# Layer B's sliding attention moved from VectorE products to tiled matmuls over runs of 32 keys

## The chip, the cores and the metric

The kernel runs on one core of one Trainium2 chip. The metric is device time of one execution in microseconds. A core has engines that work side by side and wait for each other by semaphores: TensorE (PE) for matmuls, with weight loads shown apart as PEld; VectorE (DVE) for elementwise work; ScalarE (ACT) for activations and copies; GpSimd (POOL); and SyncE (SP), whose queue issues the DMAs. TensorE writes to PSUM, eight banks of 512 float32 columns on 128 partitions, and DVE or ACT carry results from there to SBUF. On this core each engine runs its own instructions in the order in which they were written.

## The reference

Four residual layers A, B, A, B on one sequence of 2048 positions, 512 channels, 32 heads of 16. Layer A is linear attention with a learned feature map; the change touches layer B, in which each position attends to eight positions: itself and those 2, 4, ... 14 before it.

```python
x = x + _A_ref(_layernorm(x, axis=-1), A_wqkv, A_w_phi, A_wo)
x = x + _B_ref(_layernorm(x, axis=-1), B_wqkv, B_wo)
x = x + _A_ref(_layernorm(x, axis=-1), A_wqkv, A_w_phi, A_wo)
x = x + _B_ref(_layernorm(x, axis=-1), B_wqkv, B_wo)

def _B_ref(x, wqkv, wo):                       # S = 2048, H = 32, Dh = 16
    W, dil = 8, 2
    q, k, v = ...                              # x @ wqkv, by head
    idx = pos[:, None] - (jnp.arange(W) * dil)[None, :]
    mask = idx >= 0
    kg, vg = ...                               # k and v at idx: (B, H, S, W, Dh)
    logits = jnp.einsum("bhsd,bhswd->bhsw", q, kg) * Dh ** -0.5
    logits = jnp.where(mask[None, None, :, :], logits, -1e9)
    attn = _softmax(logits, axis=-1)
    o = jnp.einsum("bhsw,bhswd->bhsd", attn, vg)
    return o.transpose(0, 2, 1, 3).reshape(B, S, D) @ wo
```

## The kernel before

The sequence is cut into four blocks `b` of 512 positions, each of four tiles `t` of 128. Both rounds `L` of the layers use the same weights, held in SBUF. The stages of one round are: `s_a1` (keys and values of layer A, their features, and the running sum `kv` over all four blocks), `s_a2` (query features), `s_akv` (the finished sum turned into weights, once a round), and then for each block `s_a3` (normalisers), `s_a4` (layer A's output), `s_b1`, `s_b2`, `s_b3` (layer B). `s_out` ends both layers: four matmuls of 512 columns per tile against the output weights (L520), and the residual. The residual is added in one of two ways: by a fifth matmul with the identity and an eviction on ACT (L523, L530), or by DVE (L533). Then come sums of squares and the normalisation for the next layer.

Every step goes through `step` (a named thread of one engine) or `flex` (a copy that may run on DVE or ACT). `_ORDER`, a list of thread names written out by hand or by a search, says in which order the steps are emitted, and so the order on each engine; `_CHOICE` has one digit for each flexible step (DVE or ACT; for the residuals, identity matmul or DVE); `_SLOTS` names the buffer that each tile takes. There is no scheduler at run time.

Layer B, per block:

- `s_b1`: 48 matmuls of 512 columns at L927 give Q, K and V with channels on partitions, each a weight block of every fourth column of `WB` (so that one partition holds one head's channel). ACT or DVE evict each 128x512 result (L190, L192). POOL adds a halo of 16 positions from the block before (L953, L965, L969). Then `vrep` makes 16 DMAs (L988) that copy V, shifted, into `Vg`.
- `s_b2`: `prod` (L1019), four DVE products of 128x4096 of Q with eight shifted views of K; `lgt` (L1026), 32 matmuls with the 0/1 weights `indQK` on four column tiles of 32, which sum the channels; `ex` (L1033), two exponentials; `den` (L1042), two matmuls that sum the eight exponentials; `rd` (L1047, L1049), logarithm and exponential for the reciprocal; `pt` (L1054), the normalised weights.
- `s_b3`: `pav` (L1081), four DVE products of 128x4096 of these weights with views of `Vg`; `mo` (L1090), 32 matmuls with `indAV` that sum over the window; four evictions; `s_out`.

A matmul can use a part of the 128x128 array, given by `tile_position`: a shape such as 128x32 (rows x columns) leaves four tiles that are used in turn. L668 (`kv`) uses two tiles of 128x64, L714 (`ms`) and L782 (`md`) four of 128x32, L900 sixteen of 32x32, L808 four of 32x128.

At the start `warm` puts 14 matmuls on a zeroed tile `kvT` (L242, L287). In layer A four more blocks write and read DRAM for `rho` (L824, L831), the only round trips through DRAM of this kernel.

Of the kernel before, what the change touches and what calls it, by code (L numbers as in the profile page):

```python
# [8 lines left out]
BF16 = mybir.dt.bfloat16  # L9
# [20 lines left out]
KVW = 16 + TB  # L30
VGW = 3 * KVW + TB + 8
# [5 lines left out]
_BUFS = {"big": 8, "med": 16, "t2": 6, "ps": 8}  # L37
# [3 lines left out]
    "fold_dma": (),  # L41
    "half_k": ((0, 3), (1, 3)),
    "half_ln": (),
    "split": ((1, 2), (1, 3)),
    "v_dram": (),
    "half_mo": (),
    "rho_pad": 0,
# [10 lines left out]
av 8 i i i i i i i i i i i i 0 f 0 g e 2t 0 bs 9 h a d c 0 j k t i i j l 27 o p 3 3 d6 b 1x 1x t 1y o m 2 2 1q  # L58
1z 1x 1x q u t r 1q v x w n s 1r w 1s 4 20 y 21 1x 22 1x 23 1q 1q 1q 1q 1v 1w z 3d 3d 3d 1u 1t 25 3e 3e 3e z 5
3e 3e z z 26 10 18 18 d5 1 z 16 11 4i 15 6 1h 13 3d 3e 3e 25 25 26 18 25 18 12 26 26 28 26 26 26 26 19 12 28  # L60
2a 28 1h 18 14 12 12 1a 28 1c 3e 2g 2g 1f 2h 2h 1h 1h 1b 1i 2b 1b 1e 1d 29 2j 2k 1h 1j 1n 2r 1b 1l 2s 1b 2c 2r
1k 2s 17 2g 2g 2h 2h 1k 1k 2h 2h 2h 2h 2d 1g 2d 2d 2d 2e 2j 1m 35 36 32 2o 2o 33 2s 33 32 33 33 2r 2s 2s 1o 2o
2o 2d 2r 3a 1k 3a 1p 2p 2o 24 24 2s 24 2u 2v 35 37 2u 2u 2u 2s 2i 2w 2j 3a 2s 3a 2l 2z 2j 24 32 32 34 2m 3b 33
3d 3f 3f 2z 2z 2z 33 2f 33 33 2f 2f 2f 3a 3a 2q 2q 2q 30 3a 2n 3a 3a 2z 3e 2q 2x 35 35 b6 3b 3a 2y 31 31 31 31
3c 3c 38 3c 39 3c 3m 3f 3n 3o 3o 3o 24 24 3g 3g 3g 3f 3p 3q 3g 3g 3g 3g 3g 3r 3q 3f 3g 24 3h 3i 3i 5l 5m 5n 3p
3s 3q 3j 3k 3k 3t 3q 3p 3x 5m 3w 3u 3h 3i 3i 3q 3v 3q 3q 3y 3h 3i 3q 3i 3h 3i 3q 5l 5o 5p 5r 5m 5q 7 7 3z 3q
3i 3j 3k 5m 5l 5s 3k 7 7 5m 5m 5m 3h 3i 7g 40 5u 44 41 42 5t 5m 5m 3j 3j 7h 7i 3k 5v 5m 5w 43 7h 45 7j 45 60
3k 3k 3k 46 45 45 5y 5x 5z 61 61 48 47 47 61 49 47 4a 47 4b 62 47 4b 63 3j 4g 94 4c 45 4d 45 4e 4f 3k 45 45 61
64 63 4h 4p 65 95 7j 7j 66 4q 63 96 95 97 97 63 67 7h 63 67 69 7h 6b 4k 4k 4k 4l 4p 4r 4k 4m 4p 4p 4s 4t 7k 7n
6a 68 6c 4o 7m 50 50 4u 4u 4u 4n 4u 7l 4w 97 7o 7p 7p 7q 7s 3l 4x 7r 7r 7p 7t 7p 6o 7u 50 7r 7r 7v 6o 6j 4v 4y  # L70
4j 6o 6q 6o 4j 4z 6k 6p 6r 6j 7r 6e 6l 95 6d 95 7v 6t 6s 6f 6d 7w 6e 7z 7x 98 9b 9a 99 6g 7y 9c 6e 6j 6j 9d 9d
6u 9d 6e 6n 80 6m 9d 6h 6v 6v 9e 9h 9f 6i 9g 9f 6w 6v 6v 6w 6w 9f 9i 9f 87 88 8h 9j 9f 50 82 9j 9l 6w 6x 6x 87
87 6w 81 83 9n 6x 9k 87 8b 89 51 51 51 51 52 52 8c 8c 8e 6u 6u 6u 9m 8j 8a 8d 8c 6v 6y 3l 8f 82 9o 82 85 82 50
51 52 4z 4z 4z 9q 9q 9s 8c 6z 8g 6y 6z 9r 71 70 6y 6y 6z 6z 72 86 a0 a0 a1 73 84 8i 74 75 74 74 50 74 8i 76 8i
77 a2 76 79 53 53 54 55 54 a5 56 53 54 9v 78 76 9q 9q 76 a0 81 53 9v 9w 9p 7a 57 9v 9u a7 76 7a 9t 8j 7c 9y 54
58 59 59 59 9v 59 9x 7d 7e 5a 8j 8j 7b 7f 5c 5b 5d 5b 5b a0 8k 5e 5b 5f 8k 9z a7 5b 5f 5j 8k 8k 8l a3 5i b4 a4
b7 5h b4 b4 b4 8l 5g b5 b5 a7 b5 b5 a7 8k 8l 8j c3 8i c3 b8 c4 c4 c4 c4 a8 8m a8 a8 a8 c3 a9 a9 5k at c1 b5 a6
8m au au c1 c2 b5 c2 aw c2 c2 a8 a9 b5 b5 8n 8o 8n 8p 8m at au at at 8n 8q 8m a7 aa 8n aw 8r 8s au au au 8s 8s
8t au au 8s 8v a6 a6 8u aa 8w aa 8x 8u 8u 8u 8y ab ac ab ad a6 aa b7 8u b9 b7 c3 8y 90 92 c1 91 c1 c2 8z c2 c2
aw ay ab c2 ba ae ab af aw b0 c4 c4 b1 bc ag ag ag ag ah bc aj ak bc c1 c4 c4 bc al ax c3 ai ai ai bd b1 ai am  # L80
93 bf bi bg az bf ai am ar bf bf bg bg aq b7 bg bg bg bg bg bb an ao ag ag ap bi ag ag b1 b1 bc b2 c2 bi bn bi
bl bk as bq br br bq br br bq bq b1 br by by by by bt b3 b3 b3 b3 br be be be br br bz c5 c5 bh bj bn bn bn c5
bu c4 by by by by c6 bo by c6 c6 c5 bt bt bt bn bv c6 c6 c6 bz be bp bp bw bm bp bp c0 c0 by c6 c6 bx c0 c0 c9
c5 ca c6 cb cb cc cb cd ce cd fr fs c7 c8 c7 c8 c8 ft cc ci cf cd cg cd c7 c8 c8 fs fu c8 e2 fu ch cd e3 cd cc
cj ck e4 cd c7 c8 c8 c7 e3 e2 cm cd c8 e6 e7 fu cl cd cd cn cp co e5 e3 hb e3 cr e2 ea e9 cq hc cs e3 cs e8 e3
e3 hd eb ec e3 e3 e3 ed ct cv hc eh cs he ee cs ef cw eg ei cx ei ei cu ei cu cu cu fs cy fs fv ej cu cy d0 cz
ek d2 fw fx fz d3 cs cs fy cs cs g0 g0 g0 el ek em ek en ek d4 d1 dc g1 eo ek g2 g3 g2 dc de eo es g0 g4 dd dh
g2 g5 g2 he hc eq g6 d7 d8 d7 d7 d7 he di dc g2 dc d9 ep er hc et dn hf da db df dh dh dh hi hh hj hg hk hk hk
dj dk dl dm dm g6 g7 g9 dn dn dg ga f0 f0 hl hm hn hm ho hm ev ew f1 hk dn g8 do do hp f2 fa fc hm hq do do dp
ev ex fc gb ev f0 dp ey dn f3 f0 hm fc f4 hq ev ez fc do dp dn dq dq d6 f5 f6 dm dm eu hs gi gj gi fd gs hr fd  # L90
ht fd hu hv fd dq fe fe f5 f5 f8 f5 f9 f7 fb gk fd fe fc gn gn gp gi gi gl gm gd gd gd ge ic gf i7 i7 i9 gg i8
dr dr dt ds dr du hx hy gd dq gu dr dv gn gq gh i7 ff ia gu fb go ff fg fh fb fb eu gv gc gn i2 gr i3 hx hz hx
i7 i2 ib gv i4 hx i1 gc hw i2 i2 i5 gu i0 gu gv gv gw gt ie fg fi if i6 ie id gw if dw dx id gv gw id id ie ie
if if ig dw ff ig if ig fg fj dw e0 dw ff fg fk ie fl fm fl fn gu fl fl fp ih ih ih ih e1 ii ii ii ik ij fq dy
gt gt gt fo fo il io io io io ii im ip iq ip is ir ir ih ii in ip ip iu it ir gx ir gy gx gx gx gz gy h0 dz dz
iv gy h1 h4 gx gy h2 h4 iw iv h5 h5 h6 h7 gy h4 h3 h5 h8 h9 h7 h7 h4 h5 ha h7
# [4 lines left out]
    "0011111111111001110111111010000010010000000000000001011111101100100000110101000110000010000001110111"  # L101
    "1101011110010000110101000000000000001101011000000000100100000000000000000101111100000011011000000000"
    "0000000000001101111010000000100101011111010000011001110111000000000000000111111011101110010100101000"
    "00000000000001111001000000000000000000000000000000000000000000000000000000000001111"
)


_SLOTS = {
    "big": (
        "0123456701231231456204632073205712053720457604356704213560421356720415763215063506432506"  # L110
    ),
    "med": (
        "0123456789abcdef5837ae98eeaeae471853bc9e43cbe47199ce3185413cebf94c8f74e3581bc71931bc7f370bf9ac21584e"
        "af9c37214a0b589dec37"
    ),
    "t2": (
        "0123450123450342150132451032451032451032451302153421530421503452014520345123045130425123504321504321"
        "5043215043210451023134"
    ),
    "ps": (  # L120
# [9 lines left out]
class _Fast:  # L130

    def __init__(self, ctx, tc, A_x, A_wqkv, A_w_phi, A_wo, B_wqkv, B_wo, out):
# [16 lines left out]
        for n in ("xn", "xnT", "oT", "Eq", "rS", "kvp", "K", "QT", "Vg", "PT", "vh"):  # L149
            setattr(self, n, {})  # L150
# [1667 lines left out]
```

## Time and profile before

| what | value |
|---|---|
| median of 3 runs | 329.74 us (329.51 to 329.87) |
| profiled execution, first to last instruction (its span) | 327.5 us |
| TensorE clock granted over the span | 0.998 |
| PE / DVE / ACT busy | 310.3 / 302.2 / 279.3 us |
| layer B projections, L927, 384 matmuls | 87.6 us of PE |
| `lgt` L1026 and `mo` L1090, 528 matmuls | 34.1 us of PE |
| `prod` L1019 and `pav` L1081, 66 products | 145 us of DVE |

The span is what the profiled execution's page counts; the runs' times hold some 2 us more than it. Busy time is what an engine spent in instructions; the groups by line give it for each line and shape, with the number of instructions and the mean duration of one. Matmuls are pipelined, so the duration of one (380 ns for 512 columns) is longer than the distance to the next; the distance is read from start times or from a run of many in the chain of waits.

### The profile page before, as it was taken

How to read it: one execution, taken by the hardware profiler on the slowest of the kernel's cores; microseconds unless marked ns; L12 is line 12 of the kernel's file. 1: busy time of each engine (PE TensorE's matmuls, PEld its weight loads, DVE VectorE, ACT ScalarE, POOL GpSimd, SP SyncE). 2: the span in 40 equal slices, each digit the busy share in tenths (PEclk: the TensorE clock that was granted, in tenths of full speed). 3: DMA queues.
4: the chain of work that ended last, by engine and by line, in shares of the span. 5: the costliest groups of instructions: out<-in, count | busy, mean ns of one | idle time of the engine just before them, and what ended most of it. 6: DMA issues, size and time to landing. Idle time of an engine off the chain costs nothing. (4 is left out here: it accounts for less than half of the span.)

```text
span 327.5 us, 8033 instructions
## 1 busy us (share of the span) xinstructions
PE 310.3 (95%) x3176; PEld 149.5 (46%) x3203; DVE 302.2 (92%) x439; ACT 279.3 (85%) x634; POOL 25.3 (8%) x50
## 2 busy tenths in 40 slices
PE   7999999999999999999999999979999999999873
PEld 3655456445444444443444455644544454433221
DVE  7998995998998999899999999699999999999993
ACT  5999988998888999989999999798999996676550
POOL 4000000000021003000000000000000208400000
PEclk9999999999999999999999999999999999999999
DMA  7980000004556899998750300023436977679952
GB/s 197 380 197 3 0 2 4 2 20 120 105 148 135 152 164 133 139 121 154 137 135 1 67 3 2 4 59 90 128 58 125 179 146 134 150 139 158 166 176 92
DMA packets 37388, 35.41 MB, mean 108 GB/s; under 512 B 23008, under 2 KB 32224, under 8 KB 37344
## 3 DMA queue, kind: packets, MB, share of 16 engines
q1 hardware_dynamic: 36816, 34.81, 53.6%
q8 instruction: 27, 0.44, 0.6%
q14 instruction: 17, 0.14, 0.2%
q10 hardware_dynamic: 528, 0.02, 0.1%
HBM read 10.50 MB, written 2.36 MB: 39 GB/s over the span
## 5 line engine op out<-in xcount | busy, mean ns | idle before, releaser
L927 PE MATMUL ps<-xnT,WB 128*128 128x512 bf16 x384 | 87.6, 380 | 0.5 <-DMA xnT<-xn 0.5
L1081 DVE TENSOR_TENSOR pav<-PT,Vg 128x4096 bf16<-128x4096 bf16 (+1 forms) x34 | 72.0, 2162 | 1.5 <-DMA Vg<-V 1.0
L1019 DVE TENSOR_TENSOR prod<-QT,K 128x4096 bf16<-128x4096 bf16 x32 | 72.5, 2291 | 0.3 <-ACT QT L192 0.2
L927 PEld LDWEIGHTS <-WB 128*128 128x128 bf16 x384 | 42.3, 114 | 43.3 <-issue 5.8
L520 PEld LDWEIGHTS <-oT 128*128 128x128 bf16 x256 | 23.8, 97 | 34.5 <-ACT oT L192 5.7
L192 ACT CAST oT<-ps 128x512 bf16<-128x512 f32 (+1 forms) x60 | 32.1, 587 | 8.4 <-PE ps L1090 7.1
L706 ACT ACTIVATE Eq<-ps 128x512 bf16<-128x512 f32 x64 | 34.0, 615 | 0.7 <-PE ps L698 0.6
L520 PE MATMUL ps<-WoB,oT 128*128 128x512 bf16 x122 | 32.1, 380 | 2.4 <-ACT oT L192 2.0
L599 ACT ACTIVATE Ek<-ps 128x512 bf16<-128x512 f32 x64 | 33.6, 622 | 0.4 <-PE ps L593 0.2
L698 PE MATMUL ps<-xnT,WA 128*128 128x512 bf16 x128 | 30.7, 380 | 0.6 <-DVE Eq L816 0.6
L540 ACT ACTIVATE sqd<-x 128x512 bf16<-128x512 bf16 x48 | 30.1, 643 | 1.0 <-DVE x L533 0.8
L605 PE MATMUL ps<-WA,xnT 128*128 128x512 bf16 x120 | 30.0, 380 | 0.5 <-issue 0.2
L593 PE MATMUL ps<-WA,xnT 128*128 128x512 bf16 x124 | 29.7, 380 | 0.6 <-DMA xnT<-xn 0.2
L520 PE MATMUL ps<-WoA,oT 128*128 128x512 bf16 x120 | 29.2, 380 | 0.4
L533 DVE SCALAR_TENSOR_TENSOR x<-ps,x 128x512 bf16<-128x512 f32 x38 | 25.4, 686 | 1.9 <-PE ps L520 1.7
L192 ACT CAST V<-ps 128x512 bf16<-128x512 f32 x31 | 17.5, 595 | 4.4 <-PE ps L927 4.3
L192 ACT CAST K<-ps 128x512 bf16<-128x512 f32 x31 | 17.8, 585 | 3.7 <-PE ps L927 3.3
L530 ACT ACTIVATE x<-ps 128x512 bf16<-128x512 f32 x26 | 15.1, 598 | 6.4 <-PE ps L523 6.3
L192 ACT CAST QT<-ps 128x512 bf16<-128x512 f32 x29 | 17.1, 592 | 2.5 <-PE ps L927 2.5
L651 DVE TENSOR_TENSOR Ek<-Ek,rk 128x4096 bf16<-128x4096 bf16 (+1 forms) x10 | 18.6, 1858 | 0.5 <-ACT rk L646 0.5
L593 PEld LDWEIGHTS <-xnT 128*128 128x128 bf16 x128 | 12.1, 97 | 15.4 <-DMA xnT<-xn 0.7
L446 ACT ACTIVATE xn<-x,nmr,rstd 128x512 bf16<-128x512 bf16 x23 | 18.2, 822 | 1.0 <-DVE nmr L435 0.8
(129 smaller groups left out, 433.3 us busy)
## 6 DMA issues: line engine op xcount, KB each, us to landing
Vg<-V SPq DMA_DIRECT2D x128, 131.5 KB, 4.4
Prho<-rd SPq DMA_DIRECT2D x8, 512.0 KB
x<-in_A_x_dram SPq DMA_DIRECT2D x3, 512.0 KB
WB<-in_B_wqkv_dram SPq DMA_DIRECT2D x3, 512.0 KB, 11.6
wraw<-in_A_wqkv_dram SPq DMA_DIRECT2D x4, 256.0 KB, 4.5
out_dram<-x SPq DMA_DIRECT2D x4, 256.0 KB, 2.2
out_dram<-x SPq DMA_DIRECT2D x8, 128.0 KB, 2.2
x<-in_A_x_dram SPq DMA_DIRECT2D x4, 128.0 KB
```

The costliest lines, as they stand in the source:

```text
L192: self.nc.scalar.copy(out=out, in_=in_)
L520: nc.tensor.matmul(y[:], lhsT=oT[:, c, t * P:(t + 1) * P], rhs=Wo()[:, c, :], start=(c == 0), stop=(c == NB - 1 and not onpe))
L533: nc.vector.scalar_tensor_tensor(out=xb[:, t, :], in0=T[t][:], scalar=1.0, in1=xb[:, t, :], op0=ALU.mult, op1=ALU.add, **kw)
L540: nc.scalar.activation(out=sqd[:], in_=xb[:, t, :], func=ACT.Square, accum_out=T["ss"][:, t:t + 1])
L593: nc.tensor.matmul(pk[:], lhsT=xnT[:, t, k, :], rhs=self.WA[:, k, D:2 * D], start=(k == 0), stop=(k == NB - 1))
L599: nc.scalar.activation(out=T["E"][:, t, s, :], in_=T["k", t][:], func=ACT.Exp, scale=1.0 - 2.0 * s)
L605: nc.tensor.matmul(pv[:], lhsT=xnT[:, t, k, :], rhs=self.WA[:, k, 2 * D:3 * D], start=(k == 0), stop=(k == NB - 1))
L698: nc.tensor.matmul(pq[:], lhsT=self.WA[:, k, hb * P:(hb + 1) * P], rhs=xnT[:, :, k, :], start=(k == 0), stop=(k == NB - 1))
L706: nc.scalar.activation(out=self.Eq[L, b][s][:, :, hb, :], in_=T[hb][:].rearrange("p (t i) -> p t i", t=4), func=ACT.Exp, scale=1.0 - 2.0 * s)
L927: nc.tensor.matmul(pp[:], lhsT=self.WB[:, k, i * D + c:(i + 1) * D:NB], rhs=xnT[:, :, k, :], start=(k == 0), stop=(k == NB - 1))
L1019: nc.vector.tensor_tensor(out=pr[:], in0=QT[:, c:c + 1, :].to_broadcast([P, NW, TB]), in1=win, op=ALU.mult)
L1081: nc.vector.tensor_tensor(out=pv, in0=PT[:, :, lo:lo + n].unsqueeze(1).to_broadcast([P, NB, 2, n]), in1=vw, op=ALU.mult)
```

## The change

What is computed stays the same. Layer B's scores and weighted values are now matmuls between queries and keys themselves:

- Positions are dealt to partitions differently: a block's 512 positions are loaded and stored so that tiles 0 and 1 hold its even and tiles 2 and 3 its odd positions, so that a window (every second position) is a run of eight neighbours.
- Keys are taken in overlapping runs of 32, one for each 21 queries or so (`WS`), `NWIN` = 6 runs for each tile of 128 queries.
- `s_b1`: Q and K as before, but with contiguous weight columns; Q is then spread by eight DMAs (`qsc`) into `Qbd`, a tile in which each head's queries stand alone and all else is zero. V is projected with positions on partitions (`mv`), written to DRAM (`vwr`) and read back in runs of 32 (`vrd`, `vrd0`) into `Vbd`, again zero elsewhere. `Qbd` and `Vbd` exist once and are cleared at the start by six DVE steps.
- `s_b2`, per tile of 128 queries: `sc`, 48 matmuls on eight tiles of 64x32, for four heads at once, into a pair of PSUM banks; `ex`, one exponential of 128x1024; `msk`, one product with a 0/1 mask.
- `s_b3`, per tile: `dn`, two matmuls on two 128x64 tiles, sums; `mo`, 48 matmuls on two 128x64 tiles; `ln` and `rd` for the reciprocal; `nrm`, one DVE product that also evicts. `s_out` follows once per block.
- PSUM is one tile of eight banks, handed out singly or in pairs: layer A's exponentials, `mulp` and evictions now take two banks (1024 columns) in one instruction.
- POOL's halo copies are gone (K's halo is a DVE copy). `_ORDER`, `_CHOICE` and `_SLOTS` are new; unused options are removed. On DVE the new order begins with `mask_h`, `zero_q`, `phi`, `zero` (the `kvT` clear), `small`, `zero_v`; the 14 `warm` steps stand before the first `tr` of the weights.

The core of the diff:

```diff
+    def pp(self):
+        k = int(self.slot("pp")[2:])
+        return self.PS[:, k:k + 2, :]
...
+        def zero_q(i):
+            nc.vector.memset(self.Qbd[:, 2 * i:2 * i + 2, :, :], 0.0)
+
+        def zero_v(i):
+            nc.vector.memset(self.Vbd[:, i // 2, i % 2 * NWIN:i % 2 * NWIN + NWIN, :, :], 0.0)
...
         def ek(t, s):
-            nc.scalar.activation(out=T["E"][:, t, s, :], in_=T["k", t][:], func=ACT.Exp, scale=1.0 - 2.0 * s)
+            nc.scalar.activation(out=T["E"][:, 2 * t:2 * t + 2, s, :], in_=T["k", t][:], func=ACT.Exp,
+                                 scale=1.0 - 2.0 * s)
...
         def mm(i, c):
-                nc.tensor.matmul(pp[:], lhsT=self.WB[:, k, i * D + c:(i + 1) * D:NB], rhs=xnT[:, :, k, :],
+                nc.tensor.matmul(pp[:], lhsT=self.WB[:, k, i * D + c * P:i * D + (c + 1) * P], rhs=xnT[:, :, k, :],
                                  start=(k == 0), stop=(k == NB - 1))
+        def mv(t):
+            xnT = self.xnT["B%d" % L, b]
+            T[2, t] = pp = self.ps()
+            for k in range(NB):
+                nc.tensor.matmul(pp[:], lhsT=xnT[:, t, k, :],
+                                 rhs=self.WB[:, k, 2 * D:3 * D].rearrange("p (a e d) -> p a d e", a=NB, d=DH),
+                                 start=(k == 0), stop=(k == NB - 1))
...
+        def qsc(g):
+            lo = DH * g
+            nc.sync.dma_start(out=self.Qbd[lo:lo + DH, :, g % 4, :], in_=T[0][lo:lo + DH, :, :])
+
+        def vwr(r):
+            dst = self.VD[L][r, 256 * b:256 * b + 256, :].rearrange("(f p) d -> p f d", p=P)
+            nc.sync.dma_start(out=dst, in_=T[2][:, 2 * r:2 * r + 2, :])
+
+        def vrd(r, c):
+            w0 = 0 if b else 1
+            lo = c * DH
+            row = 256 * b - 7 + WS * w0
+            a = self.VD[L][r, row:row + 1, c * P:c * P + 1]
+            src = bass.AP(a.tensor, a.offset, [[D, 32], [WS * D, 2 * NWIN - w0], [1, P]])
+            dst = self.Vbd[32 * c:32 * c + 32, r, w0:, lo:lo + DH, :].rearrange("k j d e -> k j (d e)")
+            nc.sync.dma_start(out=dst, in_=src)
...
+        def sc():
+            S = T["S"] = self.pp()
+            K = self.K[L, b]
+            for w in range(NWIN):
+                lo, hi = self.win(t % 2, w)
+                k0 = KH - 7 + WS * (t % 2 * NWIN + w)
+                for c in range(NB):
+                    for r in range(2):
+                        o = S[32 * c:32 * c + 32, r, lo:lo + 1]
+                        out = bass.AP(o.tensor, o.offset, [list(o.ap[0]), [P, NB], [1, hi - lo]])
+                        nc.tensor.matmul(out, lhsT=K[64 * r:64 * r + 64, c, t // 2, k0:k0 + 32],
+                                         rhs=Q[64 * r:64 * r + 64, c, :, t * P + lo:t * P + hi],
+                                         start=(w == 0), stop=(w == NWIN - 1), tile_position=(64 * r, 32 * c),
+                                         skip_group_check=True)
+        def ex():
+            E = self.ET[L, b, t] = self.et()
+            nc.scalar.activation(out=E[:].rearrange("p r h q -> p r (h q)"), in_=T["S"][:], func=ACT.Exp,
+                                 scale=float(DH) ** -0.5, accum_out=self.stE[:, idx:idx + 1])
+        def msk():
+            nc.vector.tensor_tensor(out=E, in0=E, in1=m[:].unsqueeze(1).to_broadcast([P, 8, P]), op=ALU.mult)
...
+        def dn():
+            for r in range(2):
+                nc.tensor.matmul(Dn[64 * r:64 * r + 64, :], lhsT=self.oneB[:], rhs=E[:, :, r::2, :], start=True,
+                                 stop=True, tile_position=(0, 64 * r), skip_group_check=True)
+        def mo():
+            E = self.ET[L, b, t]
+            T["O"] = O = self.ps()
+            for w in range(NWIN):
+                lo, hi = self.win(t % 2, w)
+                for j in range(NB):
+                    for r in range(2):
+                        nc.tensor.matmul(O[64 * r:64 * r + 64, j * P + lo:j * P + hi],
+                                         lhsT=V[:, t // 2, t % 2 * NWIN + w, :, 2 * j + r],
+                                         rhs=E[:, j // 2, j % 2 * 2 + r, lo:hi],
+                                         start=(w == 0 and j == 0), stop=(w == NWIN - 1),
+                                         tile_position=(0, 64 * r), skip_group_check=True)
+        def ln():
+            nc.scalar.activation(out=T["l"][:], in_=T["D"][:], func=ACT.Ln, bias=self.tiny_t[:, 0:1])
+        def rd():
+            nc.scalar.activation(out=T["r"][:], in_=T["l"][:], func=ACT.Exp, scale=-1.0,
+                                 accum_out=self.stR[:, idx:idx + 1])
+        def nrm():
+            nc.vector.tensor_tensor(out=self.oT[key, b][:, :, t * P:(t + 1) * P],
+                                    in0=T["O"][:].rearrange("p (j q) -> p j q", j=NB),
+                                    in1=T["r"][:].rearrange("p (j q) -> p j q", j=NB), op=ALU.mult)
```

Tiles `Qbd` (128 x 4 x 4 x 512) and `Vbd` (128 x 2 x 12 x 64 x 8) are bfloat16; the last index of `Vbd`, of which `mo` takes one of eight, is the head within a group of eight.

More of the change, by code (lines that the diff above doesn't have):

```diff
@@ L126 @@
+    "et": (
+        "01234563120543651205364021504365"
     ),
@@ L572, in s_out @@
                 add(st, "ACT", sq, t)
-                if half and t % 2:
-                    norm(t - 1, 2)
             elif last and split:
@@ L578, in s_out @@
                 add(st, "SP", store, t - 1, t + 1)
-        if not last and not half:
+        if not last:
             norm(0, 4)
@@ L640, in t1, with rl @@
                                     op=ALU.add)
+        def rl(t, m):
+            s1 = T["s1"][:, 0:m * G]
+            nc.scalar.activation(out=s1, in_=s1, func=ACT.Ln)
         def rr(t, m):
@@ new lines, in vrd0 @@
+        def vrd0(r, c):
+            lo = c * DH
+            dst = self.Vbd[32 * c + 7:32 * c + 32, r, 0, lo:lo + DH, :].rearrange("k d e -> k (d e)")
+            nc.sync.dma_start(out=dst, in_=self.VD[L][r, 0:25, c * P:(c + 1) * P])
+        for i in range(2):
+            for c in range(NB):
+                add(st + "qk"[i], "PE", mm, i, c)
+                self.flex(st + "qk"[i], ev, i, c)
+        add(st + "k", "DVE", khalo)
+        for g in range(8):
+            add(st + "q", "SP", qsc, g)
@@ L1030, in ex @@
[L1030 to L1043 removed]
+        Q = self.Qbd
```

586 lines of the change are left out of this document (243 added, 343 removed).

## The prediction

> **What bounds the kernel now.** I read first the page's list of busy times, then its forty slices, then the waits of each engine, the chain of work that ended last, and last the groups by line with shapes apart.
>
> ```profile
> PE 310.3 (95%) x3176; PEld 149.5 (46%) x3203; DVE 302.2 (92%) x439; ACT 279.3 (85%) x634; POOL 25.3 (8%) x50
> ...
> PE   7999999999999999999999999979999999999873
> ...
> DVE  7998995998998999899999999699999999999993
> ACT  5999988998888999989999999798999996676550
> ```
>
> TensorE (PE) works without a break from the first slice to the last four; VectorE (DVE) nearly so. PE idles 327.5 - 310.3 = 17.2 us, and the windows say where: 8.7 us of it lie after 305 us and 1.7 us before 10 us.
>
> ```profile
> 0.00:10.00 10.00, 8.29 (x66) 4.78 (x67) 8.20 (x32) 6.00 (x12) 3.97 (x27) 1.00 0.79 229
> ...
> 260.00:290.00 30.00, 30.00 (x209) 14.10 (x211) 29.91 (x17) 22.84 (x45) 10.78 (x6) 1.00 0.72 141
> ...
> 305.00:327.50 22.50, 13.80 (x117) 4.43 (x117) 16.93 (x21) 8.01 (x17) 0.00 (x0) 0.98 0.58 143
> ```
>
> (After the length: PE, weight loads, DVE, ACT, POOL; clock granted, DMA share, GB/s.) Between 260 and 290 us PE and DVE are both full. The chain runs through PE alone from 230 to 290 us, and these pieces price it:
>
> ```profile
> 252.37 1.84 PE ps L1026 x32
> ...
> 277.68 0.55 PE ps L1090 x8
> ...
> 258.65 0.43 PE ps L1042 x2
> ```
>
> A 512-column matmul on the whole array takes 0.215 us (the last piece). Eight on four quarter arrays take 0.55, thirty-two 1.84: so 1.29 / 24 = 54 ns each while they run, four at once, and 0.12 us on top for changing the tile shape. PE is in order, so what counts is the sum of its work.
>
> **What goes.** Of PE: 256 L1026 and (in full-width terms) 256 L1090 matmuls at 54 ns, 13.8 us each line, and 16 of L1042, 3.5: together 31.1. (Their busy times sum to 38.6; the other 7.5 are changes of shape. Counted on the PE steps of the two order lists the shape changes 109 times before and 110 after, so that part stays.) The new choice string sends 59 instead of 38 of the 64 residual additions to DVE: 21 identity matmuls (L523) of 0.216 go, 4.5 us. Projections and output matmuls keep their count.
>
> Of DVE: `prod` 72.5, `pav` 72.3, `PT` 5.4. Of ScalarE (ACT): 34 evictions of `ps` to `oT` at 0.54 = 18. Of POOL: the halos, for which no engine but POOL waits. Of DMA: 128 x 131.5 KB = 16.8 MB.
>
> **What comes, off PE.** DVE: 32 masks of the shape of L1054 (0.687) 22.0; 32 `nrm` like L816 (0.682) 21.8; 41 more evictions in b1 and 7 in a1 and 21 residuals at 0.686, 47.3; zeroing `Qbd` and `Vbd`, 10,240 words at the 256 words in 0.272 us of L242, 10.9; masks and halos some 5. 302.2 - 150.2 + 107 = 259. ACT: 32 `ex` of 1024 elements (an eviction of 1024, L192, takes 1.07, the accumulator 0.21) 41 for 12.9; 32 logs and exponentials (0.702 + 0.631 + 0.188) 48.7 for 12.2; less the 18, 48 evictions (27) and 21 residuals (12), `bs` 4: about 283 - 6 for norms moved to DVE = 277. The paired exponentials save nothing sure: 64 x 1.07 = 68 against 67.6 us busy for 128 now. Both stay under PE's sum below, so PE hides them. Data moved falls to 4.2 (Q) + 4.2 + 6.3 (V through DRAM) = 14.7 MB.
>
> **What comes, on PE.** Small matmuls of one round, on different tiles, run beside each other:
>
> ```profile
> 64.56 0.63 PE L714 MATMUL ps<-Eq,indS 128*32 128x128 bf16 x32
> 65.00 0.63 PE L782 MATMUL ps<-Eq,ZM 128*32 128x128 bf16 x32
> ...
> 46.44 1.92 PEld L668 LDWEIGHTS <-vaug 128*33 128x33 bf16 x128 [0.42 <-issue]
> ```
>
> 32 start within 65.00 - 64.56 = 0.44 us, 14 ns each with their own weights; a round of four tiles streams its 128 columns in 55 ns.
> - *Scores* (`sc`): 48 matmuls per step, six rounds of eight tiles, about 85 columns a round, 512 in all: one 512-column matmul's 0.216 plus six small gaps and the start of eight, 0.257; x 32 steps = 8.2 us (bounds: 7; 16.4 if the two row tiles that share a strip of columns take turns). I take 8.2, since L900 (32x32, 32 instructions of 512 columns) takes 0.59 us, so row tiles do overlap.
> - *Denominators* (`dn`): two half arrays side by side, 0.219 x 32 = 7.0 (14 if not).
> - *Values* (`mo`): 48 per step, 24 rounds of two half arrays: 768 rounds. The nearest row is L668, also two half arrays: 128 loads in 1.92 us, 30 ns a round, which streams 64 columns. Here only 21 stream, but 64 weight columns are loaded instead of 33, and from every eighth element of `Vbd`. Low end 30. If loading was what filled those 30 ns, 64 columns take 58. Reading apart costs more: the one strided load of this kernel is
>
> ```profile
> L927 PEld LDWEIGHTS <-WB 128*128 128x128 bf16 x384 | 42.3, 114 | 43.3 <-issue 5.8 <-DMA xnT<-xn 1.0 <-DVE xnT L190 0.4
> L520 PEld LDWEIGHTS <-oT 128*128 128x128 bf16 x256 | 23.8, 97 | 34.5 <-ACT oT L192 5.7 <-issue 3.5 <-ACT x L530 0.4
> ...
> L1026 PEld LDWEIGHTS <-indQK 128*32 128x32 bf16 x256 | 6.0, 96 | 10.9 <-issue 6.4
> ```
>
> every fourth element: 114 ns against 97. As 128 columns take no longer than 32 (97, 96), these 17 ns belong to 32 columns' worth of time; 64 columns pay 34: high end 92. I take 44, half-way from 30 to 58: 33.8 us (23.0 to 70.7).
> - *V projection*: 128 matmuls keep 512 columns, but the moving operand is now `WB` read at every sixteenth element; before only the hidden weight load was strided. No matmul of the trace streams so. Low end 0 extra, high end the same 17 ns per 32 columns, 272 a matmul. I take half, 136: 17.4 us (0 to 34.8).
>
> The Trainium skill ("SBUF — State Buffer", section "Door 1: The DMA port swizzle") has SBUF in lines of 16 bytes and wants two hits in a line for full bandwidth; both new reads touch each line once. The trace has a price at 8 bytes only (the 17 ns); were that rule to bring both high ends, the sum below would be 411. It speaks against the change.
>
> The start: DVE is in order, and now clears half of `Qbd` (2.2 us) and builds `PHI`, for which a DMA must land, ahead of the `kvT` clear (at 0.94 us now) that the 14 warm-up matmuls wait for; they stand before the first transposes. Some 3 us (0 to 4).
>
> On SP: 160 issues at 0.59 us instead of 128; 16 of the new reads wait for V's write to land (`rd<-rho`, the like, takes 3.0 us, its longest wait 3.3), and behind each stand other reads, xnT transposes and stores. I cost it at nothing because PE has some 10 us of other work between projection and use; without that cover 3 us a block. The evictions moved to DVE and the freed DVE should shrink PE's own waits: I take 6 of the 17.2 us.
>
> **Sum:** -31.1 - 4.5 + 8.2 + 7.0 + 33.8 + 17.4 = +30.8; 327.5 + 30.8 + 3 - 6 = 355.3 span, and 2.2 more, as the median of the runs, 329.74, stands over the span: **357 us**.
>
> **Rivals.**
> - *Both strided reads run at full rate* and DVE, no longer a bound, ends the waits. Then PE's change is -35.6 + 15.2 + 23.0 = +2.6; with half of the 17.2 us of waits gone, 327.5 + 2.6 + 3 - 9 + 2.2 = 326: faster. For it: loads and matmuls of different tiles overlap wholly in L714, and the 114 ns loads of L927 never held up its 0.216 us pace. Against: that pace hides them. It decides from a V matmul under about 0.22 and a round under about 32 ns. Chance 0.28.
> - *The weight loads of `mo` bound PE at the high end*: 70.7 instead of 33.8 gives 394, with the V end 411. Chance 0.09.
> - *The round trip of V shows*: `Vbd` and `Qbd` are single, so the next block's reads wait for the last `mo`; 8 blocks x 3.0 us is 381. Against it: the page's DMA row stands at 0 to 5 tenths over long parts. Chance 0.06.
> - *The small matmuls don't overlap*: each takes its round alone. 1536 x 37 ns of scores for 8.2 and 1536 x 44 for 33.8 make +82, 439. The rows of L714 and L900 speak against it; 0.03. The Trainium skill ("TensorEngine Tiling (Array Packing)", section "Instruction Overhead") gives each matmul an overhead of some 60 cycles; one after the other at the 2.4 GHz of "TensorE: Matmul & The Clock Gate" (section "What's actually happening") that is an estimate of 25 ns, 77 us for 3072 and a total of 392. The trace's 14 ns a pair already goes against it.
>
> **Chances.** Forecast 0.54 (its own range 340 to 392). Leaving out most of the high ends and non-overlap, and below 320 a sliver of the full-rate rival, the range is 320 to 392. About 0.2% is what can be told from no change. Faster is the full-rate rival less a part near zero, 0.25; same 0.04; slower 0.71.
>
> **What would show it.** `sc` near 0.26 us and `mo` near 1.05 us a step in the rows of PE; V matmuls starting some 350 ns apart; DVE near 260, ACT near 277 us busy, PE over 96%; the first transposes about 3 us later. Wrong if V matmuls start 216 ns apart, if a `mo` step takes 0.7 us or 2.2, or if PE waits long for DMA of `Vbd`.

## The result and the profile after

The changed kernel takes 534.95 us (534.2 to 538.51, four runs) beside 329.66 us for the kernel before: a ratio of 1.6246, 95% interval 1.6192 to 1.63. The profiled execution spans 533.8 us after 327.5. The forecast was 357 us, in a range from 320 to 392.

The page's busy times and some of its slices, after:

```profile
PE 517.2 (97%) x5774; PEld 251.9 (47%) x5774; DVE 256.6 (48%) x516; ACT 276.7 (52%) x537; POOL 4.8 (1%) x29
...
PE   6999999999999999999999989999999999999993
...
DVE  7899687172512334355227859652221332323333
ACT  4999783642513466445347968544441523434260
PEclk9999997596955889697678999898876867768577
```

DVE and ACT are where they were forecast (259 and 277 us) and are no bound any more. PE alone sets the time: its idle time is 533.8 - 517.2 = 16.6 us, as little as before (17.2). New is the row of the granted clock: 9 in every slice before, now 5 to 9.

Stretches that answer to those shown of before (length; PE, weight loads, DVE, ACT, POOL; clock, DMA share, GB/s):

```profile
0.00:10.00 10.00, 4.97 (x24) 2.26 (x25) 7.64 (x18) 2.60 (x4) 3.63 (x26) 1.00 0.83 242
10.00:85.00 75.00, 73.99 (x1012) 39.27 (x1011) 64.06 (x129) 66.75 (x117) 0.78 (x2) 1.00 0.25 69
260.00:290.00 30.00, 30.00 (x310) 19.08 (x309) 13.26 (x29) 16.21 (x32) 0.00 (x0) 0.77 0.18 38
500.00:533.80 33.80, 25.72 (x307) 17.57 (x305) 11.63 (x24) 10.56 (x18) 0.00 (x0) 0.70 0.23 72
```

Up to 85 us, where layer A's first part ends, the clock is full. In layer B PE is always busy while DVE and ACT stand half idle. The chain of waits (start, length, what) prices the pieces:

```profile
82.90 3.67 PE PS L939 x4
86.57 1.71 PE PS L932 x4
88.28 7.32 PE PS L939 x8
...
102.10 3.41 PE PS L932 x8
105.51 2.44 PE PS L553 x8
107.95 2.59 PE PS L932 x12
...
112.11 5.18 PE PS L553 x24
...
162.27 5.63 PE PS L1063 x96
```

A V matmul (L939) takes 3.67 / 4 = 0.92 us, not 0.216. A round of two `mo` matmuls (L1063) takes 5.63 / 48 = 117 ns. And ordinary matmuls of 512 columns, which read nothing apart, come in two sorts: 2.59 / 12 = 0.216 us, but 3.41 / 8 = 0.426 just after V matmuls. The windows over these same pieces show the clock that goes with each:

```profile
82.90:86.57 3.67, 3.67 (x5) 0.48 (x4) 3.29 (x8) 0.54 (x1) 0.00 (x0) 0.97 0.09 18
86.57:88.28 1.71, 1.71 (x5) 0.60 (x4) 1.71 (x1) 0.59 (x1) 0.00 (x0) 0.50 0.24 91
88.28:95.59 7.31, 7.31 (x20) 0.83 (x27) 2.72 (x3) 1.93 (x5) 0.00 (x0) 0.50 0.21 50
...
102.10:105.50 3.40, 3.40 (x9) 1.18 (x8) 0.00 (x0) 2.16 (x4) 0.00 (x0) 0.50 0.07 18
...
107.95:110.54 2.59, 2.59 (x27) 1.06 (x33) 2.59 (x3) 0.59 (x1) 0.00 (x0) 1.00 0.10 21
...
162.30:167.90 5.60, 5.60 (x95) 5.57 (x94) 1.29 (x2) 1.41 (x3) 0.00 (x0) 0.50 0.01 3
```

The V matmuls take 0.917 us at a clock of 0.97 and 0.915 at 0.50: the array's clock is not what they wait for. The ordinary matmuls take twice their time exactly where the clock is 0.50, and PE is "busy" in every one of these windows.

### The profile page after: what moved, and what is told of

The parts are those of the page before. It is cut to its first block, busy times and chain, and to the rows that moved or that the text cites. A ratio compares the mean times of both kernels' runs of the same rounds, so it can differ in the third digit from the quotient of the medians.

```text
span 533.8 us, 13262 instructions
## 1 busy us (share of the span) xinstructions
PE 517.2 (97%) x5774; PEld 251.9 (47%) x5774; DVE 256.6 (48%) x516; ACT 276.7 (52%) x537; POOL 4.8 (1%) x29
## 4 chain that ended last, share of the span: by engine, by line
PE 94%; DVE 3%; issue 1%; DMA 1%; ACT 0%; DVEq 0%; ACTq 0%
PE PS L939 22%; PE PS L1063 17%; PE PS L932 15%; PE PS L553 12%; PE PS L632 6%; PE PS L619 6%; PE PS L732 5%; PE PS L1022 3%; PE PS L1053 2%; PE PS L698 2%; DVE Eq L857 1%; PE PS L493 1%; PE PS L328 1%; PE PS L749 1%; PE PS L907 1%
## 5 line engine op out<-in xcount | busy, mean ns | idle before, releaser
L939 PE MATMUL PS<-WB,xnT 128*128 128x512 bf16 x128 | 120.9, 1095 | 0.0
L1063 PEld LDWEIGHTS <-Vbd 128*64 128x64 bf16 x1536 | 94.9, 216 | 3.0 <-issue 2.1
L1063 PE MATMUL PS<-et,Vbd 128*64 128x21 bf16 (+3 forms) x1536 | 93.4, 269 | 0.0
L932 PE MATMUL PS<-xnT,WB 128*128 128x512 bf16 x256 | 84.5, 491 | 0.0
L566 DVE SCALAR_TENSOR_TENSOR x<-PS,x 128x512 bf16<-128x512 f32 x59 | 39.7, 687 | 35.9 <-PE PS L553 35.4
L1029 ACT ACTIVATE et<-PS 128x1024 bf16<-128x1024 f32 x32 | 32.7, 1024 | 39.6 <-PE PS L1022 37.5
L939 PEld LDWEIGHTS <-xnT 128*128 128x128 bf16 x128 | 14.6, 117 | 73.9 <-issue 70.5
L553 PE MATMUL PS<-WoB,oT 128*128 128x512 bf16 x128 | 37.5, 449 | 0.0
L632 PE MATMUL PS<-WA,xnT 128*128 128x512 bf16 x128 | 33.5, 403 | 0.0
L619 PE MATMUL PS<-WA,xnT 128*128 128x512 bf16 x128 | 32.5, 402 | 0.0
L553 PE MATMUL PS<-WoA,oT 128*128 128x512 bf16 x128 | 31.9, 387 | 0.4 <-DVE Eq L857 0.2
L625 ACT ACTIVATE Ek<-PS 128x1024 bf16<-128x1024 f32 x32 | 31.1, 1028 | 1.8 <-PE PS L619 1.7
L732 PE MATMUL PS<-xnT,WA 128*128 128x512 bf16 x128 | 30.2, 380 | 0.0
L208 DVE CAST Vs<-PS 128x512 bf16<-128x512 f32 x15 | 10.2, 688 | 37.9 <-PE PS L939 37.9
```

What stands on the lines that cost most here:

```text
L553: nc.tensor.matmul(y[:], lhsT=oT[:, c, t * P:(t + 1) * P], rhs=Wo()[:, c, :], start=(c == 0), stop=(c == NB - 1 and not onpe))
L566: nc.vector.scalar_tensor_tensor(out=xb[:, t, :], in0=T[t][:], scalar=1.0, in1=xb[:, t, :], op0=ALU.mult, op1=ALU.add, **kw)
L619: nc.tensor.matmul(pk, lhsT=xnT[:, t, k, :], rhs=self.WA[:, k, D:2 * D], start=(k == 0), stop=(k == NB - 1))
L625: nc.scalar.activation(out=T["E"][:, 2 * t:2 * t + 2, s, :], in_=T["k", t][:], func=ACT.Exp, scale=1.0 - 2.0 * s)
L632: nc.tensor.matmul(pv[:], lhsT=xnT[:, t, k, :], rhs=self.WA[:, k, 2 * D:3 * D], start=(k == 0), stop=(k == NB - 1))
L732: nc.tensor.matmul(pq, lhsT=self.WA[:, k, hb * P:(hb + 1) * P], rhs=xnT[:, :, k, :], start=(k == 0), stop=(k == NB - 1))
```

## The experiments

All times stand beside 329.6 to 330.4 us for the kernel before on the same chip. They are of one execution each, or the median of several where an interval is given.

**Each reading at unit step, alone and together.** The two operands that are read apart are V's moving operand (every sixteenth element of `WB`) and the weights of `mo` (every eighth of `Vbd`). Columns of V then stand in another order than their readers take.

```diff
 mv      (V matmuls)
-  rhs=self.WB[:, k, 2*D:3*D].rearrange("p (a e d) -> p a d e", a=NB, d=DH)
+  rhs=self.WB[:, k, 2*D:3*D]
 mo      (values)
-  lhsT=V[:, t//2, t%2*NWIN+w, :, 2*j+r]
+  lhsT=V[:, t//2, t%2*NWIN+w, 8*(2*j+r):8*(2*j+r)+8, :]
```

V alone:

> The changed kernel with one edit: the moving operand of the V projection is read in its natural column order (unit step) instead of every sixteenth element. V's channels then come out in another order, so the output differs from the reference; the work is the same in number and shape. Theory (each element that stands alone in its stretch of memory costs PE 1.79 ns, and the halved clock follows from the starved array): the V matmuls return from 918 to 216 ns, 128 x 0.70 = 90 us go, and part of the clock loss with them: 420 to 445 us, clock above 0.85, rounds of mo still near 115 ns. Rival (the clock falls because of the many small matmuls, not because of the slow reads): about 445 us, clock no better than 0.81 in the stages of layer B. Rival (the V matmuls are slow for their place, output or bank): no change, 535.

The weights of `mo` alone:

> The changed kernel with one edit: each weight load of mo takes 64 columns that stand next to each other in Vbd instead of every eighth (other columns than the reference needs, so the output differs; number and shape of the work are the same). Theory: a round of two loads falls from 115 ns to between 30 and 58, 768 rounds give 45 to 65 us, plus some of the clock loss: 450 to 485 us; V matmuls still 918 ns. Rival (64 columns on half arrays load slowly whatever the step): rounds stay at 115 ns, 530 to 540 us.

Both:

> Both edits together (output differs from the reference for the same two reasons). Theory: 90 + 45 to 65 us of reading go and the half clock with them, another 35 to 40 us: 335 to 360 us, granted clock above 0.95. Rival (small matmuls and shape changes lower the clock by themselves): 375 to 395 us with the clock near 0.85 and 427 ns matmuls still between the stages of layer B.

Measured: 444.1 us with V at unit step, 463.15 with `mo` at unit step, 370.26 with both. V matmuls then start 216 ns apart, and a step of `mo` (24 rounds) takes 0.76 us instead of 2.78 to 2.90, so a round takes 31 to 32 ns. The kernel with one edit keeps the other's price unchanged (V 918 ns, `mo` 117 ns a round). Of the 205 us that the change cost, 165 are these two readings together with the halved clock that comes with them; the single edits save 90.9 and 71.8 us. Both single edits came out inside what was expected. The pair did not: 370.26 us lies above the theory's 360 and below the rival's 375, though the granted clock of 0.960 is the theory's.

With both at unit step what is left, 40 us, is of another kind. The page's PE line of that kernel, four pieces of its chain (48 rounds of `mo` in 1.51 us, eight V matmuls in 1.73, and two DMAs), and the window around the last:

```profile
PE 330.5 (90%) x5736; PEld 175.2 (48%) x5774; DVE 255.0 (69%) x516; ACT 274.5 (74%) x537; POOL 4.8 (1%) x29
```

```profile
89.73 8.69 DMA Prho<-rd
...
159.06 1.51 PE PS L1063 x96
...
253.63 1.73 PE PS L939 x8
...
259.16 10.72 DMA Prho<-rd
```

```profile
259.00:270.00 11.00, 7.21 (x59) 2.82 (x52) 4.95 (x10) 4.49 (x8) 0.00 (x0) 1.00 0.81 140
```

PE is busy 20 us longer than in the kernel before (330.5 for 310.3) and idle 21 us longer (368.5 - 330.5 = 38.0 for 17.2). Where the two slow lines filled PE, waits now show: 5.0 us before the first matmul (1.3 in the kernel before), and others around the round trip of `rho` through DRAM, once in each round of the layers (PE idles for 3.7 us between 60 and 100 us and for 6.4 between 240 and 280). The end of the kernel adds little: 9.8 us idle after 350 us, for 8.7 after 305 us in the kernel before.

**How the price goes with the step.** One kernel gives each of the eight block-and-round pairs its own step of V's operand, and each block its own step of the weights of `mo` (the values read are then not those of the reference).

```diff
+VSTEP = (1, 2, 4, 8, 16, 32, 4, 8)
+MSTEP = (1, 2, 4, 8)
 mv
+  rhs=self.WB[:, k, 2*D:3*D].rearrange("p (a e d) -> p a d e", e=8, d=VSTEP[4*L+b])   # step 1: plain
 mo
+  lhsT=VF[:, t//2, t%2*NWIN+w, 0:64*MSTEP[b]:MSTEP[b]]
```

> A ruler: the changed kernel with another step of the moving operand of the V projection in each block (1, 2, 4, 8 elements in the four blocks of the first round of layers, then 16, 32, 4, 8) and of the weight loads of mo (1, 2, 4, 8 in blocks 0 to 3). The output differs from the reference, the work is the same in number and shape. Theory (it is the stretch of 16 bytes, eight elements, that counts): V matmuls at 216 ns for steps 1, 2 and 4 and at 918 for 8, 16 and 32; rounds of mo 30 to 58 ns for 1, 2, 4 and 115 for 8. Rival (price in proportion to the step): 16 costs twice what 8 costs, 32 four times. Rival (any step above 1 pays): 2 and 4 already slow.

Measured: 432.89 us in all. The chain of this kernel has undisturbed pieces at most steps (L941 is V at steps 1, 2, 4, 8; L1067 is `mo`, two loads a round, at steps 2, 4, 8):

```profile
82.67 0.86 PE PS L941 x4
...
105.61 2.88 PE PS L941 x12
...
118.97 5.44 PE PS L941 x12
...
163.68 1.52 PE PS L1067 x96
173.67 3.52 PE PS L941 x4
...
196.85 4.29 PE PS L1067 x141
...
208.69 5.66 PE PS L1067 x96
```

| step, elements of 2 bytes | 1 | 2 | 4 | 8 | 16 | 32 |
|---|---|---|---|---|---|---|
| V matmul of 512 columns, ns | 216 | 240 | 453 | 880 | 917 | 858 |
| a round of `mo`, two loads of 64 columns, ns | 31.1 | 31.6 | 58 to 61 | 114 to 118 | | |

The values at steps 16 and 32 are distances between starts in the trace. The expectation had steps 2 and 4 still at 216 ns and missed: V pays at any step above 1, and the price grows with the step up to 8 elements, that is 16 bytes, and then stays. One number fits the moving operand to within 7%: 1.79 ns each time that the read moves on to another stretch of 16 bytes (a stretch that it comes back to counts again). 512 columns touch 64 stretches at step 1 (115 ns, hidden under 216), 128 at step 2 (229), 256 at step 4 (458) and 512 from step 8 on (917). For weights a round of two loads fits 0.9 ns for each stretch of the two: 128 at step 8 (115 ns a round) and 64 at step 4 (58). That need not mean that one load pays half of what a moving operand pays. In all 768 rounds of the changed kernel the two loads start within 10 ns of each other, each on its own half of the array, and each lasts 216 ns; with both reads at unit step one lasts 114:

```profile
L1063 PEld LDWEIGHTS <-Vbd 128*64 128x64 bf16 x1536 | 94.9, 216 | 3.0 <-issue 2.1
...
L1063 PEld LDWEIGHTS <-Vbd 128*64 128x64 bf16 x1536 | 28.1, 114 | 5.8 <-issue 2.6
```

Two loads side by side at 1.79 ns for each of their 64 stretches come to the same 115 ns a round. No run has such a load alone, so which of the two it is stays open.

**V's operand alone, put into the kernel before.** Its 128 V matmuls (of the 384 at L927) take `WB` at step 16 as the moving operand; nothing else of the change is in it. What V holds is then not the reference's.

```diff
+  rhs = xnT[:, :, k, :]
+  if i == 2:
+      rhs = self.WB[:, k, 2*D:3*D].rearrange("p (a e d) -> p a d e", a=NB, d=DH)
   nc.tensor.matmul(pp[:], lhsT=self.WB[:, k, i*D+c:(i+1)*D:NB], rhs=rhs,
```

> The kernel before, with one edit: in its 128 V-projection matmuls the moving operand is 512 columns of WB read at every sixteenth element, in place of 512 neighbouring columns of the normalised input (the output then differs from the reference). No small matmul is added and the order stays. Theory (slow reading is the cause, and a starved array loses its clock): these matmuls start 918 ns apart, 128 x 0.70 = 90 us, and others near them run at 427 instead of 216 ns, 10 to 30 us: 425 to 450 us, granted clock below 0.95. Rival (the clock falls with the many small matmuls of the change): 415 to 422 us and the clock stays at 0.99. Rival (strided reading is slow only in the new kernel): 330.

Measured: 438.0 us. The two groups that the line now falls into, and two windows of layer B:

```profile
L930 PE MATMUL ps<-WB 128*128 128x512 bf16 x128 | 120.6, 1099 | 0.0
...
L930 PE MATMUL ps<-xnT,WB 128*128 128x512 bf16 x256 | 69.6, 428 | 0.0
```

```profile
80.00:100.00 20.00, 20.00 (x72) 4.75 (x71) 9.57 (x13) 9.96 (x20) 0.15 (x1) 0.71 0.38 90
100.00:120.00 20.00, 20.00 (x35) 4.41 (x34) 8.22 (x14) 6.26 (x15) 2.01 (x3) 0.67 0.11 27
```

The same edit in a kernel with another order, other shapes and other tiles brings the same price (matmuls 921 ns apart) and the same fall of the clock. It costs 108 us: 128 x 0.70 = 90 in the V matmuls, and 11 in ordinary projections and output matmuls at the halved clock (76 of them start 380 to 470 ns apart, 15.7 us over 216 ns each, against 23 and 5.0 us before); the other 7 were not taken apart. So neither the clock nor the price needs anything else of the change.

**Can the layout be had without the readings apart?** V can come out in its natural columns at unit step, since the eviction can turn columns: evictions of V cost the same turned or not (585 and 684 ns on ACT and DVE with the turn to step 2, 586 and 683 without). But `Vbd` wants each band's 16 channels apart from the next band's, so smaller steps in the weights mean shorter runs in the reads of `vd`. First with more reads: each read of `Vbd` is split into 8/VS reads of 16 x VS elements.

```diff
+VS = 4            # and 2
 ev  +  self.copy(dve, T[2][:, c, :].rearrange("p (a d g) -> p a d g", d=DH, g=VS),
     +            T[2, c][:].rearrange("p (a g d) -> p a d g", g=VS, d=DH))
 vrd +  for u in range(8 // VS):
     +      src = bass.AP(a.tensor, a.offset + u*DH*VS, [[D, 32], [WS*D, 2*NWIN - w0], [1, DH*VS]])
 mo  +  lhsT=V[:, t//2, t%2*NWIN+w, (2*j+r)//VS, :, (2*j+r)%VS]
```

Step 4:

> The changed kernel with both reads mended and the reference's output: WB's V columns are read in their natural order, the eviction puts V's channels into the order that Vbd wants, and Vbd keeps the heads in two groups of four, so that a weight load takes every fourth element; each V read is two DMAs. Theory (price by 16-byte stretches): V matmuls 216 ns, rounds of mo 58 ns, 20 us more than the version with every second element: 385 to 395 us. Rival (any step costs 115): 410 or more.

Step 2:

> The same with four groups of two heads, so that a weight load takes every second element, and four DMAs for each V read (256 issues more at about 0.4 us on SP). Theory: rounds of mo 31 to 32 ns; within 10 us of the version with both reads at unit step (370). Rival (SP's 100 us of added issues now set when Vbd is ready): 385 or more, with PE waiting for Vbd.

Step 2, and the constants' instructions at the start in the order of before:

> The same as fix2 with four DVE steps moved in the order list: the kvT clear first, PHI after the first statistics, and the two early clears of Qbd and Vbd to where the others stand. Theory (the start was late by the clear and by PHI's DMA): the first transposes come at 6.4 to 7 us instead of 10.9, and the time falls by 3 to 4.5 us against fix2. Rival (other work hides the late start): no change.

Measured: 400.5 us at step 4, and 469.07 at step 2: the smaller step is the slower kernel. At step 4 V matmuls are 216 ns apart and most rounds of `mo` take 58 to 60 ns, as the table of steps has it; the time is 5.5 us over what was expected. At step 2 the rival came true. The page of step 2, its chain by line and the line of `mo`:

```profile
PE 45%; SPq 22%; DMA 11%; DVE 10%; issue 6%; ACT 5%; DVEq 0%; ACTq 0%
SPq L987 16%; PE PS L1071 7%; PE PS L554 6%; PE PS L620 6%; PE PS L633 6%; PE PS L933 5%; PE PS L733 5%; DMA Prho<-rd 4%; DMA Vbd<-vd 4%; SPq L971 2%; ACT sqd L574 2%; DVE x L567 2%; SPq L994 2%; PE PS L699 2%; PE PS L1030 2%
...
L1071 PE MATMUL PS<-et,Vbd 128*64 128x21 bf16 (+3 forms) x1536 | 43.9, 199 | 51.5 <-DMA Vbd<-vd 47.9
```

PE now stands still for 47.9 us until a DMA of `Vbd` lands, and behind these DMAs stands SP's queue: 256 issues of L987 that take 132 us of its time (mean 516 ns; 64 issues and 30 us in the changed kernel, 128 and 65 at step 4). The start moved as meant (first transposes at 7.1 us instead of 10.2), and the time did not (468.69). (The next expectation speaks of 100 us in which PE waited for `Vbd`; that is all of PE's idle time, 467.3 - 367.1, and the wait for `Vbd` is the 47.9.)

Then with as many reads as in the change. The copy of V in DRAM is skewed: the piece u of row n lies at 64 x VS x (8/VS x n + 21u), so windows (21 rows apart) and pieces have one common stride, and one read brings them all.

```diff
 vwr +  dst = bass.AP(a.tensor, a.offset, [[D, P], [WS*64*VS, 8//VS], [1, 64*VS]])
 vrd +  src = bass.AP(a.tensor, a.offset, [[D, 32], [WS*64*VS, 8//VS*(2*NWIN - w0)], [1, DH*VS]])
```

Unit step, runs of 32 bytes:

> This run computes the whole reference with both readings at unit step and without more reads on SP: V comes out in its natural columns, the eviction of V turns them to (eight, band, d), the copy in DRAM lies skewed (the run of 64 of row n and eighth e at 64 x (8n + 21e), so that windows, 21 rows apart, and eighths have one common stride), and each of the 64 reads into Vbd brings 32-byte runs that stand where the weights want them. The question is why the repair with step 2 took 469 us. Theory A, SP's issues: there 256 reads left SP at 0.51 us each, SP's queue held 22% of the chain and PE waited 100 us for Vbd; here the reads are 64 again (and 32 writes for 16), so the time is that of the kernel with both unit steps, 370 us, to 385, mo rounds 31 ns, V matmuls 216 ns apart, and PE waits for Vbd under 10 us in all. Theory B, short runs: the runs here are half as long as there (32 for 64 bytes) and twice as many (some 130,000 more packets at 8 to 10 ns more each, worked out from the three kernels after, step 4 and step 2: 65,824, 91,392 and 142,528 packets in 2263, 2513 and 2909 us of engine time), so PE waits for Vbd as long as there or longer and the time is 440 us or more. Rival to both: DRAM writes in 128-byte runs make vd late; then PE waits for Vbd, but SP's queue shows waits for vd.

The same with the start of before:

> As the skewed kernel, with the constants' instructions at the start back in the order of before (the clear of kvT first, the masks and the clears of Qbd and Vbd later). If the start costs what the trace of both unit steps shows (the first transposes at 10.9 us for 6.4), the first transposes are at about 7 us and the time is 2 to 5 us under the skewed kernel's. In the pair with step 2 they moved from 10.2 to 7.1 us, and the time stayed (469.1 and 468.7): if that was SP's queue hiding it, it shows here; if the start is made up for later in any case (the first layer's engines catch up), the time is within 1 us of the skewed kernel's.

Step 2, runs of 64 bytes:

> The whole reference again, the copy of V in DRAM skewed as before (64 reads, 32 writes), but the weights at step 2, so that each read brings runs of 64 bytes: the same runs as in the pair with step 2 (469 us, 256 reads) and twice those of the skewed kernel at unit step (444.7 us, 64 reads, 266,000 packets). It tells the number of issues from the length of the runs. Theory A, the number of SP's issues: 64 for 256 at the same runs, so near the kernel with both unit steps (370 us, and 1 us for loads of 31.6 for 31.1 ns): 372 to 390 us. Theory B, the length of the runs: the same runs and as slow as there, 450 us or more. Both together (an SP issue lasts longer the more runs it holds: 0.51 us for 384 runs in the pair with step 2, 1.4 to 1.75 us for 3,072 runs in the skewed kernel): 1,536 runs an issue, some 0.8 to 1 us each, 64 of them some 30 us of SP behind 130 us before, so 385 to 425 us. mo rounds 31.6 ns and V matmuls 216 ns apart in any case.

Measured: 444.74 us at unit step (ratio 1.3489, interval 1.3458 to 1.3519), 446.08 with the start of before, and 385.12 at step 2 (ratio 1.1646, interval 1.1614 to 1.1678). At unit step the time is that of theory B (440 or more), at step 2 it fits theory A (372 to 390) and the lower end of both together (385 to 425); the earlier start gains nothing (the four runs of the skewed kernel span 443.97 to 447.44). Neither the number of issues nor the length of the runs explains all three kernels alone. At unit step SP issues few reads, but each takes long (mean 1.31 us, 84 us for the 64), as in this part of SP's timeline:

```profile
140.76 4.16 SPq L988 DMA_DIRECT2D Vbd<-vd  x3
144.96 1.64 SPq L970 DMA_DIRECT2D Qbd<-Qs  x1
146.69 1.25 SPq L979 DMA_DIRECT2D vd<-Vs  x2
147.99 7.02 SPq L988 DMA_DIRECT2D Vbd<-vd  x4
```

At step 2 they take 0.76 us each, 48 us in all. With the same 64-byte runs 64 reads instead of 256 save 84 us of time (469.07 to 385.12); with the same 64 reads, runs of 64 instead of 32 bytes save 60 (444.74 to 385.12). SP's time in these reads grows with both, and so does the time of the kernel. How much of the 60 us is SP's issuing and how much the transfers themselves wasn't separated: at unit step the 16 DMA engines are busy for 56.9% of the span (49.7% at step 2, 38.9% with 256 reads), and landings of `Vbd` hold 8% of the chain beside 11% for SP's issues of L988. The skewed kernels also write V with 32 DMAs instead of 16. The kernel with skew and step 2 is the fastest one found that computes all of the reference, and it stays 16% above the kernel before.

**The start, where nothing hides it.** The kernel with both unit steps, with the start of before:

> The kernel with both unit steps (370 us; V's columns are in another order than its readers take them, so the output is not the reference's) with the constants' instructions at the start back in the order of before. There PE sat idle to 5.0 us and the first transposes came at 10.9 us. If the start is worth what the prediction gave it, 3 us (0 to 4), the first transposes are at 7 us and the time 366 to 368 us. If it is made up for later, as in the two pairs run so far (the transposes 3 us earlier and the time the same within 1.4 us), the time is 369.5 to 371 us.

Measured: 362.02 us against 370.26, below both ranges that were expected. The first transposes are at 6.9 us instead of 10.9. That is 4 us; the rest of the 8 shows in the halved matmuls, 18 of them (3.8 us over 216 ns each) against 54 (11.5 us). These are single runs, and why fewer were halved isn't shown.

## Why the prediction was wrong

The sign was right, and so was the list of what bounds the kernel: PE's sum. The forecast span was 355.3 us, the measured one is 533.8: 178.5 more. Worked out from distances between starts of matmuls in the trace:

| term | forecast, us | measured, us | missing |
|---|---|---|---|
| V projection at step 16 | +17.4 (0 to 34.8) | 128 x 0.702 = +89.9 | 72.5 |
| `mo`, round of two | 33.8 (23.0 to 70.7) | 91.3 | 57.5 |
| projections and output matmuls at half the clock | 0 | 35.2 (170 of 896), before 5.0 | 30.2 |
| `sc` | 8.2 | 16.3 | 8.1 |
| `dn` | 7.0 | 10.4 | 3.4 |
| idle PE, the later start included | 17.2 + 3 - 6 = 14.2 | 16.6 | 2.4 |

Together 174.1 of the 178.5.

**The step that failed** is the price of the two readings, and in it one inference: that the 17 ns by which the strided load of L927 exceeds the plain loads belong to "32 columns' worth of time", and that this could be carried on to the new reads as a high end. The measured price goes with the stretches of 16 bytes, not with columns. The load of L927, 128 columns at step 4, has 64 of them: by the table of steps an estimate of 58 ns at 0.9 each, or 115 at 1.79. Either is hidden under the 216 ns of its matmul, so that the row could not show what such a read costs where nothing hides it. Why the load lasts just 114 ns isn't shown. Both "high ends" built on it, 92 ns a round and 272 a V matmul, lay under what was measured (117, and 702 extra). "Take half" between the ends made it worse; even the whole high ends would have given 411. The second step that failed is a term that the sum did not have: the halved clock, 30 us.

**The rival named** for it, `mo` and V at the high end, was the right mechanism with too small a size. The Trainium skill ("SBUF — State Buffer", section "Door 1: The DMA port swizzle") was said to speak against the change, and it did: its 16-byte line is what the table shows, as the price stops growing at a step of 16 bytes. Its figure for full bandwidth, two hits in a line, is not borne out by these reads: at step 4 two elements of each line are used, and the V matmul takes 453 ns instead of 216.

**The halved clock** was not foreseen. The prediction watched the clock (0.998 before) and counted a starved PE as a busy one. Of the ordinary projections and output matmuls of the changed kernel, 144 of 209 start 380 to 470 ns apart in the first three microseconds after the last V or `mo` matmul, 17 of 55 in the fourth, 6 of 77 in the fifth, and none of the 218 from there to the fifteenth. The Trainium skill ("TensorE: Matmul & The Clock Gate", section "What's actually happening") ties half the clock to idle windows of some 3.4 us. The 0.426 us and the length of the after-effect agree with it; but none of the windows shown over these pieces has PE idle. The trace's records of the granted clock say more. It is only ever 1.0 or 0.5 there, and from its first change on it changes only at multiples of 3.413 us. In the changed kernel 38 such stretches were filled to 85% or more by V and `mo` matmuls, and each was followed by a stretch at 0.5. Of 85 that these matmuls filled to less than 45%, 84 were followed by one at full clock; in the other PE stood still, at the end of the kernel. In between it went either way (19 times 0.5, 12 times full). So one stretch of slow reads halves the clock of the next, whatever is read in that next one. The runs suggest that an array waiting for its operand counts as idle for the gate; that is an inference from the rows, since no run shows what the gate counts.

**What held.** DVE 256.6 (259), ACT 276.7 (277), first transposes at 9.4 us after 6.4 (+3), `dn` at full clock 217 to 228 ns a step (219), and the V round trip: PE's waits for `Vbd` in the changed kernel are none that the trace shows. Two half-array matmuls do overlap: a round of `mo` at unit step takes 31 to 32 ns, as the low end had it (30).

**What was off in size.** `sc` takes 464 ns a step at its fastest, not 257. That is near the bound of 16.4 us in all, 512 ns a step, that the prediction had for row tiles that take turns and set aside because of L900; whether they do take turns wasn't tried. The rival with both reads at full rate, 326 us, was tried by itself: 370.26 us, and 362.02 with the start of before. It failed for two reasons. Its new PE lines cost more than what they replace. In that last kernel:

```profile
L1065 PE MATMUL PS<-et,Vbd 128*64 128x21 bf16 (+3 forms) x1536 | 27.8, 179 | 2.7 <-issue 2.5 <-DMA Vbd<-vd 0.2
L1024 PE MATMUL PS<-Qbd,K 64*32 64x84 bf16 (+3 forms) x1536 | 17.0, 208 | 4.4 <-issue 4.4
L1055 PE MATMUL PS<-et,oneB 128*64 128x512 bf16 x64 | 10.7, 389 | 0.0
```

27.8 + 17.0 + 10.7 = 55.5 us of PE for 38.6 before, +16.9 where the rival had 38.2 - 31.1 = +7.1. And its waits did not shrink by 9 us but grew: PE is idle for 360.2 - 327.3 = 32.9 us instead of 17.2. So "the freed DVE should shrink PE's own waits" failed too. In the kernel with both unit steps the round trip of `rho` is on the chain for 19 us; whether an order made for faster PE steps would hide it wasn't tried.

## What to carry to other kernels

Price an operand read apart by how often the read moves on to another stretch of 16 bytes, and price it where it is streamed: a strided weight load that hides under a matmul can't price a strided moving operand, or loads that come every 30 ns. Read the granted clock beside PE's busy share, since a full PE row can be an array that waits, and then the neighbours pay too. A layout that takes the stride out of a matmul moves it to a DMA; before building it, count the issues and the runs that the queue then has to carry.

## What the runs showed of the hardware

- A moving operand of bf16 cost PE about 1.79 ns for each move to another 16-byte stretch; from a step of 8 elements on the price no longer grew (880, 917, 858 ns for 512 columns at steps 8, 16, 32). At step 16 it didn't depend on the granted clock: 0.917 us at 0.97 and 0.915 at 0.50.
- A round of two loads of 64 columns on two half arrays, started together, took 31 to 32 ns at steps 1 and 2, 58 to 61 at step 4 and 114 to 118 at step 8.
- The granted clock was 1.0 or 0.5 and changed only at multiples of 3.413 us: after each of 38 such stretches filled to 85% or more with slow reads it was 0.5, though PE's row was full. Matmuls that read at unit step took 0.426 us instead of 0.216 for up to 5 us after the last slow read.
- An issue of a read of `Vbd` on SP's queue took a mean of 0.47 to 0.54 us with up to 384 runs of 64 to 256 bytes in it, 0.76 us with up to 1,536 runs of 64 bytes, and 1.31 us with up to 3,072 runs of 32 bytes.
